# Two tiles of 112 rows in place of two of 128 for each expert, in a DeltaNet layer followed by a mixture of experts

## The chip, the core and the metric

The kernel runs on one core of a Trainium2 chip. A core has five engines that work side by side and meet at semaphores: TensorE (PE; its weight loads are shown apart as PEld), VectorE (DVE), ScalarE (ACT), GpSimd (POOL) and SyncE (SP), which issues most transfers. The metric is device time in microseconds of one execution. The kernel before takes 697.7 us, the median of three runs (694.72, 697.7 and 702.56).

## The reference

The first half is a DeltaNet recurrence over 768 steps for 4 batches of 8 heads of 48 values. Its output, seen as 3072 tokens of 384 values, is `x` of the second half: a gate picks one of 4 groups, a second gate one of the 4 experts of that group, and the token goes through that one expert's two matrices.

```python
# per step t:  y = q_t . state;  state += beta_t * k_t (x) (v_t - k_t . state)   (k normalised)
g_idx = np.argmax(x @ w_group, axis=1)                # 4 groups
e_idx = np.argmax(xg @ w_expert[g], axis=1)           # 4 experts of the group
h  = np.maximum(xg[mask_e] @ w1[g, e], 0.0)           # 384 -> 1024
ye = h @ w2[g, e]                                     # 1024 -> 384
out[tok_idx] = (g_weight * e_weight)[:, None] * ye
```

How many tokens an expert gets depends on the data. Counted from the reference on its inputs, the 16 experts get 203, 162, 176, 211, 203, 190, 203, 201, 181, 200, 183, 224, 195, 202, 155 and 183 tokens.

## The kernel before

**First half.** The recurrence is worked in 24 chunks of 32 steps. Every chunk is a sequence of small matmuls (`gram`, `advance`) with a triangular inverse on DVE beside them (`inverse`), in an order that is written out by hand. `logits` and `route` follow the chunks: they compute the gates, and for each token a slot number. POOL then writes the token's row of 386 values (384 of `x`, the weight of its gate, its row number) by an indirect transfer into the table `x_dram` in device memory (L412). Every expert has a region of that table with room for all tokens; slot numbers count up from the region's first row, so an expert's tokens lie packed at its head. Early in the first half SP writes zeros over the first 256 rows of every region (L498 to L502): a row that no token fills keeps weight 0 and a row number that the last transfer skips.

**Between the halves.** `last` holds where every expert's tokens end; L512 to L519 turn this into the number of 128-row tiles beyond the static ones and their running sum, `tot_i`.

**Second half.** For every expert `take` (L525) fetches the static rows as `xg`, two or three experts ahead, and `experts_rows` (L536) works on them. `STATIC` is 2 here: two tiles of 128 rows.

- L543: PE transposes each tile in three pieces of 128 columns into `t_ps`, and DVE copies it to `xt` (L545).
- L551: the first matrix. The weights are held in the array, 128 columns of `w1` at a time, and both tiles stream past together as 256 columns of `xt`. ACT applies Relu to two such results at a time (L554).
- L558: the second matrix, with the roles exchanged. 128 tokens of `hid` are held, and 384 columns of `w2` stream past; so the two tiles are apart here, with eight matmuls each.
- L561: DVE multiplies by the gate's weight, and POOL sends the rows to their tokens' places by an indirect transfer (L562). It drops rows whose number is out of bounds.

The scheduler moves the transposes ahead: PE transposes the second tile of the next expert and the first tile of the one after it in one go, right behind the last L558 of an expert. The weights of expert e+2 are issued when expert e has used its own (`load_expert`, L102, two buffers each). Every f32 matmul stands in the trace as two MATMUL records and two weight loads; a transpose as one.

**Overflow.** The loop at L577 runs `n_over` times, once for each 128-row tile beyond the static ones: it picks the expert, fetches its weights again, and works on one tile.

Of the kernel before, what the change touches and what calls it, by code (L numbers as in the profile page):

```python
# [9 lines left out]
I32 = mybir.dt.int32  # L10
# [6 lines left out]
RG = 4  # L17
LEAD = 9
ACT_STEP, PE_STEP = "ScalarE", "TensorE"
XW = 386  # L20


def constants(n_tokens, seq, n_experts, n_group, n_batch):

    import numpy as np

    p = np.arange(128)
    i, k = np.meshgrid(np.arange(C), np.arange(C), indexing="ij")
    first = np.arange(n_experts) * n_tokens
    out = {  # L30
        "ident": (p[:, None] == p[None, :]),
        "upper": np.concatenate([(i < k).astype(np.float32)] * n_batch, axis=0),
        "below": np.tile(-(i > k).astype(np.float32).reshape(1, C * C), (128, 1)),
        "before": (p[:, None] < p[None, :]),
        "ones": np.ones((128, 128)),
        "desc": np.tile(np.arange(n_group, 0, -1), (128, RG)),
        "rowid": ((p // C) * seq + p % C)[:, None] - n_tokens,
        "first": (p[:, None] == 0) * first[None, :],
        "tile": np.tile(first // 128, (128, 1)),
        "expert": np.tile(np.arange(n_experts), (128, 1)),  # L40
        "part": p[:, None],
        "tiny": np.full((128, 1), 1e-36),
        "eps": np.full((128, 1), 1e-6),
    }
# [8 lines left out]
def deltanet_then_moe(  # L53
    ctx: ExitStack,
    tc: tile.TileContext,
    const_at: dict,
    shape: tuple,
    kq_d: bass.AP,
    kv_d: bass.AP,
# [28 lines left out]

    x_dram = dp.tile([NE * NS, 128, XW], F32, name="x_dram")

# [20 lines left out]
    with ExitStack() as first:  # L111
# [34 lines left out]
        nc.gpsimd.tensor_copy(acc[:, 0], cut["first"])  # L146
        zero = ap_.tile([128, STATIC * XW], F32, name="zero")
        nc.gpsimd.memset(zero, 0.0)
# [211 lines left out]
        def route(r):  # L360
# [46 lines left out]
            for g, u in enumerate(us):  # L407
                x = xs.pop(u)
                nc.gpsimd.tensor_copy(x[:, DM:DM + 1], cw[:, g])
                for _ in range(2):  # L410
                    yield
                put = nc.gpsimd.indirect_dma_start(  # L412
                    out=x_dram.rearrange("t p d -> (t p) d"),
                    out_offset=bass.IndirectOffsetOnAxis(ap=slot_i[:, g], axis=0),
                    in_=x[:, :], in_offset=None).ins
# [36 lines left out]
        with tc.manual_schedule(engines={mybir.EngineType.PE, mybir.EngineType.DVE,  # L452
# [16 lines left out]
            for u in range(NCH + 1):  # L469
# [28 lines left out]
                if u == 1:  # L498
                    for e in range(NE):
                        nc.sync.dma_start(  # L500
                            out=x_dram[e * NS:e * NS + STATIC].rearrange("t p d -> p t d"),
                            in_=zero.rearrange("p (t d) -> p t d", t=STATIC))  # L502
            while behind:
# [7 lines left out]
        tiles_i = cp.tile([128, NE], I32, name="tiles_i")  # L511
        nc.vector.tensor_scalar(tiles_i, last, 127.0, None, op0=ALU.add)  # L512
        nc.vector.tensor_scalar(tiles_i, tiles_i, 7, None, op0=ALU.arith_shift_right)
        nc.vector.tensor_copy(over, tiles_i)
        nc.vector.tensor_tensor(over, over, cut["tile"], op=ALU.subtract)
        nc.vector.tensor_scalar(over, over, -float(STATIC), 0.0, op0=ALU.add, op1=ALU.max)
        nc.vector.tensor_tensor_scan(out=incl, data0=cut["ones"][:, 0:NE], data1=over,
# [6 lines left out]

    def take(rows, n):  # L525

        xg = mp.tile([128, n, XW], F32, tag=f"xg{n}", name="xg", bufs=3)
        nc.sync.dma_start(out=xg, in_=rows.rearrange("t p d -> p t d"))
        return xg

    def places(xg, n):
        at = mp.tile([128, n], I32, tag=f"at{n}", name="at", bufs=4)
        nc.vector.tensor_scalar(at, xg[:, :, DM + 1], float(N), None, op0=ALU.add)  # L533
        return at

    def experts_rows(xg, T, w1, w2):  # L536

        at = places(xg, T)
# [7 lines left out]
        hid = mp.tile([128, FC, T * 128], F32, tag="hid", name="hid")  # L546
        for f in range(0, FC, 2):
            h_ps = ps.tile([128, 2, T * 128], F32, tag="h", name="h_ps", bufs=3)
            for k in range(2):
                for j in range(DC):  # L550
                    nc.tensor.matmul(h_ps[:, k], lhsT=w1[:, j, (f + k) * 128:(f + k + 1) * 128],  # L551
                                     rhs=xt[:, j], start=(j == 0), stop=(j == DC - 1),
                                     skip_group_check=True)
            nc.scalar.activation(hid[:, f:f + 2], h_ps, ACT.Relu)  # L554
        for i in range(T):
            y_ps = ps.tile([128, DM], F32, tag="o", name="y_ps")
            for f in range(FC):
                nc.tensor.matmul(y_ps, lhsT=hid[:, f, i * 128:(i + 1) * 128], rhs=w2[:, f],  # L558
                                 start=(f == 0), stop=(f == FC - 1))
            yo = mp.tile([128, DM], F32, tag="yo", name="yo", bufs=4)  # L560
            nc.vector.tensor_scalar(yo, y_ps, xg[:, i, DM:DM + 1], None, op0=ALU.mult)  # L561
# [3 lines left out]

    static = lambda e: take(x_dram[e * NS:e * NS + STATIC], STATIC)
    ready = {0: static(0), 1: static(1)}
    for e in range(NE):
        if e + 2 < NE:
            ready[e + 2] = static(e + 2)  # L570
        experts_rows(ready.pop(e), STATIC, *weights.pop(e))
        if e + 2 < NE:
# [4 lines left out]
    with tc.For_i(0, n_over):  # L577
# [6 lines left out]
        nc.vector.tensor_tensor(col, taken, col, op=ALU.subtract)  # L584
        nc.vector.scalar_tensor_tensor(col, in0=ef, scalar=float(NS), in1=col, op0=ALU.mult,
                                       op1=ALU.add)
        pick = mp.tile([128, 2], I32, name="pick")
        nc.vector.tensor_copy(pick[:, 0:1], ef)
        nc.vector.tensor_scalar(pick[:, 1:2], col, float(STATIC), None, op0=ALU.add)
        nc.vector.tensor_scalar(taken, taken, 1.0, None, op0=ALU.add)  # L590
# [3 lines left out]
        cv = nc.values_load(pick[0:1, 1:2], engines=[mybir.EngineType.SP], min_val=0,  # L594
                            max_val=NE * NS - 1,
                            skip_runtime_bounds_check_because="a tile of the sorted tokens")
# [4 lines left out]
        row, used = mp.tile([128, 1], F32, name="row"), mp.tile([128, 1], F32, name="used")  # L601
        nc.vector.tensor_scalar(row, col, float(STATIC), 128.0, op0=ALU.add, op1=ALU.mult)
        nc.vector.tensor_tensor(row, row, cut["part"], op=ALU.add)
        nc.vector.tensor_tensor(used, row, lim, op=ALU.is_lt)
        nc.vector.tensor_scalar(used, used, float(NE * N), None, op0=ALU.mult)
# [11 lines left out]
        experts_rows(take(x_dram[ds(cv, 1)], 1), 1, w1, w2)  # L617

# [44 lines left out]
```

## Time and profile before

| | |
|---|---|
| median of 3 runs | 697.7 us (694.72 to 702.56) |
| the profiled execution | 697.92 us, span 696.1 us |
| PE busy | 549.5 us (79%) |
| PEld busy | 429.6 us (62%) |
| DVE, ACT, POOL busy | 260.0, 138.6, 82.9 us |
| mean granted TensorE clock | 0.904 |
| transfers | 93.53 MB, mean 134 GB/s |

The span is the time from the first to the last instruction of the profiled execution; its own time is 1.8 us longer. "Busy" is the time in which an engine had an instruction under way. Two instructions on PE overlap, so a busy PE doesn't say how fast it goes: that is read from how many instructions of a form lie in how long a stretch. PEclk or "clock" is the share of full speed that TensorE was granted; 1.00 is 2.4 GHz and 0.50 is 1.2 GHz.

### The profile page before, as it was taken

The numbers are of one execution on the slowest core, as the hardware profiler recorded it, in microseconds if no ns is written. First come the engines' busy times: TensorE is split into PE (matmuls) and PEld (weight loads), VectorE is DVE, ScalarE is ACT, GpSimd is POOL, SyncE is SP. The second block draws the span as 40 slices with busy tenths as digits, with TensorE's granted clock in tenths as the row PEclk, the third lists the DMA queues.
The fourth block names the chain that finished last, engine by engine and source line by source line (L and its number), as shares of the span: only waits on it lengthen the run. The fifth ranks groups of instructions, "written<-read, shape, count | busy, mean of one in ns | idle before, by whom it ended". The sixth has DMA issues, their size and how long they took to land. (4 is left out here: it accounts for less than half of the span.)

```text
span 696.1 us, 20147 instructions
## 1 busy us (share of the span) xinstructions
PE 549.5 (79%) x9170; PEld 429.6 (62%) x9170; DVE 260.0 (37%) x773; ACT 138.6 (20%) x233; POOL 82.9 (12%) x152
## 2 busy tenths in 40 slices
PE   2403576777877788861999999999999999999994
PEld 1303465667666677751776677766776677766772
DVE  4399865977859897222111100110001100111000
ACT  1201233343443543320110011101110011100110
POOL 4000000011113103224011100110011100111001
PEclk9999778886868878875999999999999999999997
DMA  9980854233312112103246354553646445463200
GB/s 231 299 251 26 250 170 154 75 93 94 95 48 72 50 48 95 50 14 126 86 159 212 115 205 158 194 181 142 210 135 217 146 178 189 153 217 121 92 5 17
DMA packets 42374, 93.53 MB, mean 134 GB/s; under 512 B 3608, under 2 KB 28362, under 8 KB 42288
## 3 DMA queue, kind: packets, MB, share of 16 engines
q1 hardware_dynamic: 38704, 82.76, 37.0%
q0 software_dynamic: 3584, 9.47, 3.7%
q8 instruction: 72, 1.18, 0.7%
q14 instruction: 14, 0.11, 0.1%
HBM read 76.43 MB, written 17.36 MB: 135 GB/s over the span
## 5 line engine op out<-in xcount | busy, mean ns | idle before, releaser
L551 PE MATMUL h_ps<-xt,w 128*128 128x256 f32 x768 | 170.6, 382 | 8.1 <-DVE xt L545 8.1
L558 PE MATMUL y_ps<-w,hid 128*128 128x384 f32 x512 | 167.7, 486 | 0.0
L551 PEld LDWEIGHTS h_ps<-xt,w 128*128 128x128 f32 x768 | 145.1, 191 | 31.0 <-DVE xt L545 11.7
L558 PEld LDWEIGHTS y_ps<-w,hid 128*128 128x128 f32 x512 | 97.3, 190 | 64.4
L561 DVE TENSOR_SCALAR yo<-y_ps,xg 128x384 f32<-128x384 f32 x32 | 19.7, 617 | 226.3 <-PE y_ps L558 226.3
L554 ACT ACTIVATE hid<-h_ps 128x512 f32<-128x512 f32 x64 | 38.2, 597 | 322.9 <-PE h_ps L551 322.9
L562 POOL DMA_INDIRECT out_dram<-yo,at x32 | 31.5, 983 | 331.2 <-DVE yo L561 327.0
L227 DVE TENSOR_TENSOR m<-m,t 128x30 f32<-128x30 f32 (+9 forms) x180 | 59.5, 330 | 4.5
L223 DVE TENSOR_TENSOR t<-m 128x30 f32<-128x30 f32 (+9 forms) x180 | 59.3, 330 | 4.6
L166 PE MATMUL g_ps<-kqt 48*32 48x64 f32 x1536 | 26.8, 271 | 22.4 <-issue 9.9
L289 ACT ACTIVATE s_bd<-s_ps 48x768 f32<-48x768 f32 x46 | 37.0, 805 | 30.6 <-PE s_ps L282 30.0
L533 DVE TENSOR_SCALAR at<-xg 128x2 int32<-128x2 f32 x16 | 2.7, 168 | 101.5 <-DMA xg<-x_dram 101.5
L282 PE MATMUL s_ps<-w,kv 32*48 32x48 f32 x1472 | 25.9, 227 | 17.1 <-issue 12.3
L355 PE MATMUL l_ps<-wr,xt 128*128 128x20 f32 x144 | 25.0, 304 | 15.7 <-DVE gq L174 10.4
L166 PEld LDWEIGHTS g_ps<-kqt 48*32 48x32 f32 x1536 | 20.7, 129 | 26.6 <-issue 11.8
L271 PE MATMUL w_ps<-f,mt 32*32 32x48 f32 x1472 | 23.1, 213 | 15.9 <-DVE f L259 15.3
L282 PEld LDWEIGHTS s_ps<-w,kv 32*48 32x48 f32 x1472 | 21.7, 134 | 21.2 <-issue 14.2
L293 PE MATMUL o_ps<-w,gq 32*32 32x48 f32 x1536 | 31.8, 250 | 3.1 <-issue 3.1
L255 PE MATMUL a_ps<-s_bd,kqt 128*32 128x96 f32 x736 | 31.9, 337 | 2.5 <-issue 1.7
L355 PEld LDWEIGHTS l_ps<-wr,xt 128*128 128x128 f32 x144 | 22.3, 231 | 18.2 <-DVE gq L174 11.8
L271 PEld LDWEIGHTS w_ps<-f,mt 32*32 32x32 f32 x1472 | 19.5, 112 | 21.5 <-DVE f L259 17.9
L293 PEld LDWEIGHTS o_ps<-w,gq 32*32 32x32 f32 x1536 | 27.2, 141 | 4.5 <-issue 3.6
(92 smaller groups left out, 404.0 us busy)
## 6 DMA issues: line engine op xcount, KB each, us to landing
w<-in_w_dram SPq DMA_DIRECT2D x32, 1536.0 KB, 7.2
kqt<-in_kq_dram SPq DMA_DIRECT2D x48, 192.0 KB, 5.9
kv<-in_kv_dram SPq DMA_DIRECT2D x24, 384.0 KB, 3.4
x_dram<-zero SPq DMA_DIRECT2D x16, 386.0 KB, 8.7
xg<-x_dram SPq DMA_DIRECT2D x16, 386.0 KB, 7.5
con<-in_const_dram SPq DMA_DIRECT2D x1, 754.0 KB, 5.8
out_dram<-yo,at POOLq DMA_INDIRECT x32, 6.2
x_dram<-x,slot_i POOLq DMA_INDIRECT x24, 2.9
```

The lines of the kernel that those rows point to most:

```text
L166: nc.tensor.matmul(g_out[quads[b], hh, j], lhsT=kqt[rows, 0, j, quads[b]], rhs=kqt[rows, :, j, quads[b]], start=True, stop=True, skip_grou ...
L223: nc.vector.tensor_tensor(tv, m[:, j + 1:, j:j + 1].to_broadcast([128, n, j]), m[:, j:j + 1, 0:j].to_broadcast([128, n, j]), op=ALU.mult)
L227: nc.vector.tensor_tensor(m[:, j + 1:, 0:j], m[:, j + 1:, 0:j], tv, op=ALU.add)
L255: nc.tensor.matmul(a_ps[quads[b], 2 * j:2 * j + 2, :], lhsT=kqt[:, 0, j, quads[b]], rhs=s_bd[:, b, j], start=True, stop=True, skip_group_c ...
L271: nc.tensor.matmul(w_ps[b, h], lhsT=mt[b, uu * H + (h % 2) * NP + h // 2], rhs=f[b, h], start=True, stop=True, skip_group_check=True)
L282: nc.tensor.matmul(s_at[hh * 64:hh * 64 + D, b, j], lhsT=k[quads[b], 2 * j + hh], rhs=w[quads[b], 2 * j + hh], start=(u == 0 and j == 0), ...
L289: nc.scalar.activation(s_bd[rows, :, :, hh, :], s_at[rows], ACT.Copy)
L293: nc.tensor.matmul(o_ps[b, h], lhsT=gq[b, h % 2, h // 2], rhs=w[b, h], start=(u == 0 and h == 0), stop=True, skip_group_check=True)
L355: nc.tensor.matmul(l_ps, lhsT=xt[:, j], rhs=wr[:, j], start=(j == 0), stop=(j == DC - 1))
L551: nc.tensor.matmul(h_ps[:, k], lhsT=w1[:, j, (f + k) * 128:(f + k + 1) * 128], rhs=xt[:, j], start=(j == 0), stop=(j == DC - 1), skip_grou ...
L554: nc.scalar.activation(hid[:, f:f + 2], h_ps, ACT.Relu)
L558: nc.tensor.matmul(y_ps, lhsT=hid[:, f, i * 128:(i + 1) * 128], rhs=w2[:, f], start=(f == 0), stop=(f == FC - 1))
```

## The change

Every expert has 224 static slots (`SLOTS`) in place of 256. They are worked as two tiles of `P` = 112 rows. `slots(e)` views them so that partition p holds the slots 2p and 2p+1, one piece of 772 values of the table, where before it held the slots p and 128+p, two pieces of 386. All shapes of `experts_rows` follow from `xg`: the transposes give 112 columns, L551 streams 224, L558 holds 112 tokens and streams 384 columns of `w2` as before.

A region of the table now has `room` = 3200 rows in place of 3072, and the table is addressed in units of 32 rows, since 224 is no multiple of 128. A tile of the overflow loop still has 128 rows, and begins at unit 7 of the region. The number of those tiles is 0 for up to 224 tokens, and 1 for 225 to 352. One small DVE instruction between the halves is gone (L515): the constant `full` takes in what was subtracted twice.

```diff
+SLOTS = 224
-        "tile": np.tile(first // 128, (128, 1)),
+        "full": np.tile(first + SLOTS - 127, (128, 1)),
-    STATIC = -(-N // (NE * 128))
+    T, P = 2, SLOTS // 2
-    x_dram = dp.tile([NE * NS, 128, XW], F32, name="x_dram")
+    x_dram = dp.tile([NE * room // 32, 32, XW], F32, name="x_dram")
+    def slots(e):
+        rows = x_dram[e * room // 32:(e * room + SLOTS) // 32].rearrange("a b d -> (a b) d")
+        return rows.rearrange("(p t) d -> p t d", t=T)
...
-                        nc.sync.dma_start(
-                            out=x_dram[e * NS:e * NS + STATIC].rearrange("t p d -> p t d"),
-                            in_=zero.rearrange("p (t d) -> p t d", t=STATIC))
+                        nc.sync.dma_start(out=slots(e), in_=zero.rearrange("p (t d) -> p t d", t=T))
...
-        nc.vector.tensor_scalar(tiles_i, last, 127.0, None, op0=ALU.add)
+        nc.vector.tensor_tensor(tiles_i, last, cut["full"], op=ALU.subtract)
         nc.vector.tensor_scalar(tiles_i, tiles_i, 7, None, op0=ALU.arith_shift_right)
         nc.vector.tensor_copy(over, tiles_i)
-        nc.vector.tensor_tensor(over, over, cut["tile"], op=ALU.subtract)
-        nc.vector.tensor_scalar(over, over, -float(STATIC), 0.0, op0=ALU.add, op1=ALU.max)
+        nc.vector.tensor_scalar(over, over, 0.0, None, op0=ALU.max)
...
-        xt = mp.tile([128, DC, T * 128], F32, tag="xt", name="xt")
+        xt = mp.tile([128, DC, T * P], F32, tag="xt", name="xt")
         for i in range(T):
-            t_ps = ps.tile([128, DC, 128], F32, tag="t", name="t_ps")
+            t_ps = ps.tile([128, DC, P], F32, tag="t", name="t_ps")
             for j in range(DC):
                 nc.tensor.transpose(out=t_ps[:, j], in_=xg[:, i, j * 128:(j + 1) * 128],
-                                    identity=ident)
-            nc.vector.tensor_copy(xt[:, :, i * 128:(i + 1) * 128], t_ps)
+                                    identity=ident[0:P, 0:P])
+            nc.vector.tensor_copy(xt[:, :, i * P:(i + 1) * P], t_ps)
...
-            h_ps = ps.tile([128, 2, T * 128], F32, tag="h", name="h_ps", bufs=3)
+            h_ps = ps.tile([128, 2, T * P], F32, tag="h", name="h_ps", bufs=3)
...
-            y_ps = ps.tile([128, DM], F32, tag="o", name="y_ps")
+            y_ps = ps.tile([P, DM], F32, tag="o", name="y_ps")
             for f in range(FC):
-                nc.tensor.matmul(y_ps, lhsT=hid[:, f, i * 128:(i + 1) * 128], rhs=w2[:, f],
+                nc.tensor.matmul(y_ps, lhsT=hid[:, f, i * P:(i + 1) * P], rhs=w2[:, f],
                                  start=(f == 0), stop=(f == FC - 1))
```

No instruction changes its place on an engine. PE, one expert and the head of the next, in the order of the program before (the last numbers are output partitions x columns and how many in a row; `w_14` with the lower number behind it is `w1` of expert 14):

```order
L543 MATMUL t_ps<-con,xg 128x128 x6
L551 MATMUL h_ps<-xt,w_14_6790 128x256 x24
L558 MATMUL y_ps<-w_14_6791,hid 128x384 x16
L543 MATMUL t_ps<-con,xg 128x128 x3
L551 MATMUL h_ps<-xt,w_15_6870 128x256 x24
```

And the same place of the change:

```order
L545 MATMUL t_ps<-con,xg 128x112 x6
L553 MATMUL h_ps<-xt,w_14_6791 128x224 x24
L560 MATMUL y_ps<-w_14_6792,hid 112x384 x16
L545 MATMUL t_ps<-con,xg 128x112 x3
L553 MATMUL h_ps<-xt,w_15_6871 128x224 x24
```

The counts stay; the columns that stream past fall in L543 and L551, and in L558 only the output's partitions do.

DVE between the halves before, from the tokens' ends to the first copy of `xt`:

```order
L512 TENSOR_SCALAR tiles_i<-last 128x16
L405 CAST slot_i<-slot 128x4
L513 TENSOR_SCALAR tiles_i<-tiles_i 128x16
L514 CAST over<-tiles_i 128x16
L515 TENSOR_TENSOR over<-over,con 128x16
L516 TENSOR_SCALAR over<-over 128x16
L517 SCALAR_TENSOR_TENSOR incl<-con,over 128x16
L519 CAST tot_i<-incl 128x1
L533 TENSOR_SCALAR at<-xg 128x2
L545 COPY xt<-t_ps 128x3x128
```

And in the change:

```order
L517 TENSOR_TENSOR tiles_i<-last,con 128x16
L412 CAST slot_i<-slot 128x4
L518 TENSOR_SCALAR tiles_i<-tiles_i 128x16
L519 CAST over<-tiles_i 128x16
L520 TENSOR_SCALAR over<-over 128x16
L521 SCALAR_TENSOR_TENSOR incl<-con,over 128x16
L523 CAST tot_i<-incl 128x1
L540 TENSOR_SCALAR at<-xg 112x2
L547 COPY xt<-t_ps 128x3x112
```

One instruction is gone ahead of L517 of before, and the copies have 112 columns a piece.

## Rows read from the trace of the kernel before

**Rows 1.** Windows by stage: us, then each engine's busy us (instructions), clock, transfers.

```profile
0.00:62.00 62.00, 12.01 (x576) 9.07 (x576) 38.55 (x92) 6.98 (x12) 7.45 (x18) 1.00 0.78 219
62.00:326.00 264.00, 190.12 (x7218) 166.02 (x7218) 184.03 (x602) 93.39 (x157) 43.99 (x102) 0.78 0.30 93
326.00:332.00 6.00, 1.79 (x8) 1.44 (x9) 1.08 (x4) 0.00 (x0) 0.00 (x0) 0.50 0.65 202
354.00:686.00 332.00, 323.63 (x1287) 236.83 (x1285) 34.34 (x73) 35.83 (x60) 29.48 (x30) 1.00 0.46 157
686.00:697.00 11.00, 0.00 (x0) 0.00 (x0) 0.39 (x1) 0.00 (x0) 0.98 (x1) 0.62 0.03 9
```

**Rows 2.** Timeline of PE and DVE over one expert: start, length in us, count.

```profile
508.61 0.82 PE L543 MATMUL t_ps<-con,xg 128*128 128x128 f32 x6
509.94 10.63 PE L551 MATMUL h_ps<-xt,w 128*128 128x256 f32 x48 [0.52 <-DVE xt L545]
520.41 10.48 PE L558 MATMUL y_ps<-w,hid 128*128 128x384 f32 x32
530.73 0.49 PE L543 MATMUL t_ps<-con,xg 128*128 128x128 f32 x3
...
508.81 0.62 DVE L561 TENSOR_SCALAR yo<-y_ps,xg 128x384 f32<-128x384 f32 x1 [4.54 <-PE y_ps L558]
509.34 1.01 DVE L545 COPY xt<-t_ps 128x384 f32<-128x384 f32 x2
```

**Rows 3.** Timeline of PE, 511 to 519 us: 39 matmuls of L551.

```profile
510.69 8.58 PE L551 MATMUL h_ps<-xt,w 128*128 128x256 f32 x39
```

**Rows 4.** Groups by line and form, second half: busy us, mean ns, idle before.

```profile
L551 PE MATMUL h_ps<-xt,w 128*128 128x256 f32 x768 | 170.6, 382 | 8.1 <-DVE xt L545 8.1
L558 PE MATMUL y_ps<-w,hid 128*128 128x384 f32 x512 | 167.7, 486 | 0.0
L551 PEld LDWEIGHTS h_ps<-xt,w 128*128 128x128 f32 x768 | 145.1, 191 | 31.0 <-DVE xt L545 11.7
L558 PEld LDWEIGHTS y_ps<-w,hid 128*128 128x128 f32 x512 | 97.3, 190 | 64.4
L554 ACT ACTIVATE hid<-h_ps 128x512 f32<-128x512 f32 x64 | 38.2, 597 | 322.9 <-PE h_ps L551 322.9
L561 DVE TENSOR_SCALAR yo<-y_ps,xg 128x384 f32<-128x384 f32 x32 | 19.7, 617 | 226.3 <-PE y_ps L558 226.3
L545 DVE COPY xt<-t_ps 128x384 f32<-128x384 f32 x32 | 16.4, 548 | 1.2 <-PE t_ps L543 1.2
L357 DVE COPY lg<-l_ps 128x20 f32<-128x20 f32 x24 | 4.2, 176 | 30.6 <-PE l_ps L355 30.5
L516 DVE TENSOR_SCALAR over<-over 128x16 f32<-128x16 f32 x1 | 0.2, 174 | 0.0
```

**Rows 5.** L543: duration min/median/max in ns, first and last start.

```profile
L543 PE MATMUL t_ps<-con,xg x96: 272/273/455, 330.2 to 663.7; 128*128 128x128 f32 x96
```

**Rows 6.** Timeline near 307 us: six weight loads of 128 columns for 20-column matmuls.

```profile
306.99 0.74 PEld L355 LDWEIGHTS l_ps<-wr,xt 128*128 128x128 f32 x6 [0.88 <-ACT xt L351]
```

**Rows 7.** Timeline of SP: the two weight transfers that one expert releases.

```profile
520.60 0.37 SPq L105 DMA_DIRECT2D w<-in_w_dram  x1
530.92 0.37 SPq L106 DMA_DIRECT2D w<-in_w_dram  x1
```

**Rows 8.** Transfers by kind: count, KB each, median us from issue to landing.

```profile
w<-in_w_dram SPq DMA_DIRECT2D x32, 1536.0 KB, 7.2
x_dram<-zero SPq DMA_DIRECT2D x16, 386.0 KB, 8.7
xg<-x_dram SPq DMA_DIRECT2D x16, 386.0 KB, 7.5
out_dram<-yo,at POOLq DMA_INDIRECT x32, 6.2
```

**Rows 9.** Timeline of the zeros' issue (SP), and of what PE waits for then.

```profile
26.43 16.03 SPq L500 DMA_DIRECT2D x_dram<-zero  x15
...
62.72 1.50 PE L271 MATMUL w_ps<-vh,mt 32*32 32x48 f32 x64 [29.12 <-DVE vh L240]
```

**Rows 10.** Timeline between the halves.

```profile
319.37 0.17 DVE L516 TENSOR_SCALAR over<-over 128x16 f32<-128x16 f32 x1
319.65 1.03 POOL L412 DMA_INDIRECT x_dram<-x,slot_i  x1 [2.10 <-DVE over L516]
324.06 0.97 POOL L412 DMA_INDIRECT x_dram<-x,slot_i  x1 [0.28 <-POOL x L409]
326.89 1.41 SPq L528 DMA_DIRECT2D xg<-x_dram  x3
330.06 0.17 DVE L533 TENSOR_SCALAR at<-xg 128x2 int32<-128x2 f32 x1 [10.11 <-DMA xg<-x_dram]
```

**Rows 11.** Timeline of the end.

```profile
685.77 0.62 DVE L561 TENSOR_SCALAR yo<-y_ps,xg 128x384 f32<-128x384 f32 x1 [4.54 <-PE y_ps L558]
686.67 0.98 POOL L562 DMA_INDIRECT out_dram<-yo,at  x1 [4.18 <-DVEq L577]
```

More of the change, by code (lines that the diff above doesn't have):

```diff
@@ L18, with constants @@
 LEAD = 9
+SLOTS = 224
 ACT_STEP, PE_STEP = "ScalarE", "TensorE"
 XW = 386
-def constants(n_tokens, seq, n_experts, n_group, n_batch):
+def constants(n_tokens, seq, n_experts, n_group, n_batch, room):
     import numpy as np
@@ L28, in constants @@
     i, k = np.meshgrid(np.arange(C), np.arange(C), indexing="ij")
-    first = np.arange(n_experts) * n_tokens
+    first = np.arange(n_experts) * room
     out = {
@@ L57, in deltanet_then_moe @@
     shape: tuple,
+    room: int,
     kq_d: bass.AP,
@@ L79, in deltanet_then_moe @@
     NS = N // 128
-    STATIC = -(-N // (NE * 128))
+    T, P = 2, SLOTS // 2
+    assert room % 32 == 0 and SLOTS % 32 == 0 and room >= N + 128
     assert B * C == 128 and NCH % RG == 0
@@ L146, in deltanet_then_moe @@
         nc.gpsimd.tensor_copy(acc[:, 0], cut["first"])
-        zero = ap_.tile([128, STATIC * XW], F32, name="zero")
+        zero = ap_.tile([P, T * XW], F32, name="zero")
         nc.gpsimd.memset(zero, 0.0)
@@ L412, in route @@
                 put = nc.gpsimd.indirect_dma_start(
-                    out=x_dram.rearrange("t p d -> (t p) d"),
+                    out=x_dram.rearrange("a b d -> (a b) d"),
                     out_offset=bass.IndirectOffsetOnAxis(ap=slot_i[:, g], axis=0),
@@ L523, in deltanet_then_moe, with take, experts_rows @@
     ps = ctx.enter_context(tc.tile_pool(name="ps_moe", bufs=2, space=PSUM))
[L525 to L532, printed above, removed]
+    def take(rows):
+        p, t, _ = rows.shape
+        xg = mp.tile([128, t, XW], F32, tag=f"xg{t}", name="xg", bufs=3)
+        nc.sync.dma_start(out=xg[0:p], in_=rows)
+        at = mp.tile([128, t], I32, tag=f"at{t}", name="at", bufs=4)
+        return xg[0:p], at[0:p]
+    def experts_rows(xg, at, w1, w2):
+        P, T, _ = xg.shape
         nc.vector.tensor_scalar(at, xg[:, :, DM + 1], float(N), None, op0=ALU.add)
-        return at
-    def experts_rows(xg, T, w1, w2):
-        at = places(xg, T)
-        xt = mp.tile([128, DC, T * 128], F32, tag="xt", name="xt")
+        xt = mp.tile([128, DC, T * P], F32, tag="xt", name="xt")
         for i in range(T):
-            t_ps = ps.tile([128, DC, 128], F32, tag="t", name="t_ps")
+            t_ps = ps.tile([128, DC, P], F32, tag="t", name="t_ps")
             for j in range(DC):
                 nc.tensor.transpose(out=t_ps[:, j], in_=xg[:, i, j * 128:(j + 1) * 128],
-                                    identity=ident)
-            nc.vector.tensor_copy(xt[:, :, i * 128:(i + 1) * 128], t_ps)
-        hid = mp.tile([128, FC, T * 128], F32, tag="hid", name="hid")
+                                    identity=ident[0:P, 0:P])
+            nc.vector.tensor_copy(xt[:, :, i * P:(i + 1) * P], t_ps)
+        hid = mp.tile([128, FC, T * P], F32, tag="hid", name="hid")
         for f in range(0, FC, 2):
-            h_ps = ps.tile([128, 2, T * 128], F32, tag="h", name="h_ps", bufs=3)
+            h_ps = ps.tile([128, 2, T * P], F32, tag="h", name="h_ps", bufs=3)
             for k in range(2):
@@ L555, in experts_rows @@
         for i in range(T):
-            y_ps = ps.tile([128, DM], F32, tag="o", name="y_ps")
+            y_ps = ps.tile([P, DM], F32, tag="o", name="y_ps")
             for f in range(FC):
-                nc.tensor.matmul(y_ps, lhsT=hid[:, f, i * 128:(i + 1) * 128], rhs=w2[:, f],
+                nc.tensor.matmul(y_ps, lhsT=hid[:, f, i * P:(i + 1) * P], rhs=w2[:, f],
                                  start=(f == 0), stop=(f == FC - 1))
-            yo = mp.tile([128, DM], F32, tag="yo", name="yo", bufs=4)
+            yo = mp.tile([P, DM], F32, tag="yo", name="yo", bufs=4)
             nc.vector.tensor_scalar(yo, y_ps, xg[:, i, DM:DM + 1], None, op0=ALU.mult)
@@ L564, in experts_rows @@
                 in_=yo[:, :], in_offset=None, bounds_check=N - 1, oob_is_err=False)
-    static = lambda e: take(x_dram[e * NS:e * NS + STATIC], STATIC)
-    ready = {0: static(0), 1: static(1)}
+    ready = {0: take(slots(0)), 1: take(slots(1))}
     for e in range(NE):
         if e + 2 < NE:
-            ready[e + 2] = static(e + 2)
-        experts_rows(ready.pop(e), STATIC, *weights.pop(e))
+            ready[e + 2] = take(slots(e + 2))
+        experts_rows(*ready.pop(e), *weights.pop(e))
         if e + 2 < NE:
@@ L584, in deltanet_then_moe @@
         nc.vector.tensor_tensor(col, taken, col, op=ALU.subtract)
-        nc.vector.scalar_tensor_tensor(col, in0=ef, scalar=float(NS), in1=col, op0=ALU.mult,
-                                       op1=ALU.add)
+        nc.vector.tensor_scalar(col, col, 4.0, float(SLOTS // 32), op0=ALU.mult, op1=ALU.add)
+        nc.vector.scalar_tensor_tensor(col, in0=ef, scalar=float(room // 32), in1=col,
+                                       op0=ALU.mult, op1=ALU.add)
         pick = mp.tile([128, 2], I32, name="pick")
         nc.vector.tensor_copy(pick[:, 0:1], ef)
-        nc.vector.tensor_scalar(pick[:, 1:2], col, float(STATIC), None, op0=ALU.add)
+        nc.vector.tensor_copy(pick[:, 1:2], col)
         nc.vector.tensor_scalar(taken, taken, 1.0, None, op0=ALU.add)
@@ L594, in deltanet_then_moe @@
         cv = nc.values_load(pick[0:1, 1:2], engines=[mybir.EngineType.SP], min_val=0,
-                            max_val=NE * NS - 1,
+                            max_val=NE * room // 32 - 4,
                             skip_runtime_bounds_check_because="a tile of the sorted tokens")
@@ L601, in deltanet_then_moe @@
         row, used = mp.tile([128, 1], F32, name="row"), mp.tile([128, 1], F32, name="used")
-        nc.vector.tensor_scalar(row, col, float(STATIC), 128.0, op0=ALU.add, op1=ALU.mult)
+        nc.vector.tensor_scalar(row, col, 32.0, None, op0=ALU.mult)
         nc.vector.tensor_tensor(row, row, cut["part"], op=ALU.add)
         nc.vector.tensor_tensor(used, row, lim, op=ALU.is_lt)
-        nc.vector.tensor_scalar(used, used, float(NE * N), None, op0=ALU.mult)
+        nc.vector.tensor_scalar(used, used, float(NE * room), None, op0=ALU.mult)
         free, zero = mp.tile([128, 1], I32, name="free"), mp.tile([128, XW], F32, name="zero")
@@ L609, in deltanet_then_moe @@
         nc.gpsimd.indirect_dma_start(
-            out=x_dram.rearrange("t p d -> (t p) d"),
+            out=x_dram.rearrange("a b d -> (a b) d"),
             out_offset=bass.IndirectOffsetOnAxis(ap=free, axis=0), in_=zero[:, :],
-            in_offset=None, bounds_check=NE * N - 1, oob_is_err=False)
+            in_offset=None, bounds_check=NE * room - 1, oob_is_err=False)
         w1 = wp.tile([128, DC, F], F32, tag="w1", name="w1_over")
@@ L616, in deltanet_then_moe @@
         nc.sync.dma_start(out=w2, in_=w2_d[ds(ev, 1)].rearrange("o (c p) f -> p (o c) f", p=128))
-        experts_rows(take(x_dram[ds(cv, 1)], 1), 1, w1, w2)
+        rows = x_dram[ds(cv, 4)].rearrange("a b d -> (a b) d")
+        experts_rows(*take(rows.rearrange("(p t) d -> p t d", t=1)), w1, w2)
 def kernel(**inputs):
@@ L642 @@
     wr = np.concatenate([wg, we.transpose(1, 0, 2).reshape(DM, G * Eg)], axis=1)
-    const, const_at = constants(B * S, S, G * Eg, Eg, B)
+    room = -(-(B * S + 128) // 32) * 32
+    const, const_at = constants(B * S, S, G * Eg, Eg, B, room)
     ins = dict(
@@ L659 @@
     with _tile.TileContext(nc) as tc:
-        deltanet_then_moe(tc, const_at, (B, H, S, D), *args)
+        deltanet_then_moe(tc, const_at, (B, H, S, D), room, *args)
     r = _run(nc, [arrays], core_ids=[0])
```

## The prediction

> **What bounds the kernel now.** I read the windows by stage first [rows 1]. Up to 326 us DVE and PE share the first half, and nothing there is changed but the zeros. From 354 to 686 us PE is busy for 323.63 of 332 us at clock 1.00, while DVE, ACT and POOL are busy for a tenth of it each: the second half is PE's, and only what shortens PE's queue there shortens it.
>
> The timeline of one expert [rows 2] shows what an expert costs: the transposes of one begin at 508.61 us, those of the next at 530.73 us, 22.12 us. In it are 48 matmul records of L551 in 10.63 us, 32 of L558 in 10.48 us, and a turn of about 1.3 us (508.61 to 509.94) in which PE transposes and then waits for `xt`.
>
> Mean durations in the groups by line mislead here, since matmuls overlap; the distance from one start to the next is what counts. L551 with 256 columns: 39 starts in 8.58 us [rows 3], the last lasting 0.38 us [rows 4], so (8.58 − 0.38) / 38 = 215.8 ns. L558 with 384 columns: (10.48 − 0.486) / 31 = 322.4 ns [rows 2, 4]. Transposes with 128 columns: (0.82 − 0.273) / 5 = 109 ns [rows 2, 5]. From 256 to 384 columns this is 106.6 ns for 128 columns, 0.833 ns a column; and going down 128 columns from 215.8 gives 109.2 ns, which is what the transposes have. So the distance is a straight line in the columns that stream past, at full clock.
>
> **L551: 256 to 224 columns.** 224 lies between two of those points. 32 columns fewer at 0.833 ns are 26.7 ns, so 215.8 becomes 189.1 ns. There are 768 records [rows 4]: 768 × 26.7 ns = **20.5 us**, all on the path.
>
> Could the weight load become the limit? L551's own record of 128 columns lasts 191 ns [rows 4], just above 189. If a load had to end before the next began, the distance would stay near 191 and the gain would be 768 × 24.8 ns = 19.0 us. But six such loads behind each other for matmuls of 20 columns take 0.74 us [rows 6]: one begins every (0.74 − 0.19) / 5 = 110 ns, so the 191 ns overlap. I take 20.5 and keep 19.0 as an end.
>
> The Trainium skill, "TensorE: Matmul & The Clock Gate", section "Back-to-back issue gap", says that in a stream of weight loads and matmuls the spacing is about 81 ns at 128 columns and 131 ns at 512; by that a column is worth 0.13 ns, 32 of them 4.2 ns, and the sum would be an estimate of 3.2 us in place of 20.5. The rows above have 0.833 ns a column in just such a stream, so I don't use it; what a spacing of that kind would do here is a rival below.
>
> **L558: nothing.** Here the tokens are the held operand. 384 columns of `w2` stream past as before, and 322.4 ns is on the line of columns alone. 112 in place of 128 held columns shorten the load, on which PE does not wait: PEld idles for 64.4 us in this group [rows 4]. Half of the second half's matmul time thus gets nothing from fewer rows. If that cover were gone, the load would come up as a limit only at 190 ns, far under 322.
>
> **The turn between experts.** PE's first matmul of L551 waits for DVE: 8.1 us in all [rows 4], about 0.5 us for each of 15 experts. In rows 2 DVE does `yo` (0.62 us), then two copies, 0.47 us apart in start; PE goes on at 509.94, when the first copy ends (509.34 + 0.55 = 509.89), so the second, which is for the expert after, is hidden. `yo` keeps its 384 values per partition. The copy goes from 384 to 336. Between L357's 20 values in 176 ns and L545's 384 in 548 ns [rows 4] a value costs 372 / 364 = 1.02 ns, so a copy loses 49 ns; 16 × 49 = **0.8 us**. The ends are 0, if something else holds PE, and 1.6, with both copies on the path. The transposes get shorter too, 6 × 13 ns an expert, but the copy then still has `yo` ahead of it on DVE, so I count nothing. Relu on ACT (0.6 us) sits beside PE with 322.9 us to spare [rows 4].
>
> **Between the halves.** The last indirect writes start at 319.65 us, right behind L516 of DVE (319.37 + 0.17) [rows 10]. Without L515 that comes one small instruction earlier, at most 0.2 us (0.17 us by its neighbour L516, rows 4). Then come the first takes: 3.2 us from their issue to the first instruction that reads (326.89 to 330.06). Each moves an eighth less in half as many pieces. Proportion gives 0.4 us less; nothing says that time goes by bytes, so the ends are 0 and 0.4, and the same worse if longer pieces spread badly over the 16 transfer engines. Both together: **0.4 us**, between −0.4 and 0.6.
>
> **Transfers.** SP takes the zeros in 16 us from 26.43 us on, and PE's next wait is for DVE until 62.72 us [rows 9]; they are hidden, whatever they cost. The weights of expert e+2 are released at 520.60 and 530.92 us [rows 7], land in 7.2 us [rows 8], and are used more than 20 us later, after a whole other expert. An expert shorter by 1.3 us takes nothing from that, at a transfer share of 0.46 [rows 1].
>
> **The end.** From the last `yo` at 685.77 us on [rows 11] there is one indirect write of 112 rows in place of 128; I count nothing.
>
> **Sum.** 20.5 + 0.8 + 0.4 = 21.7 us, and 697.92 − 21.7 = **676.2 us**. The profiled execution lies 0.2 us above the median, so against the median of 697.7 this is the same within what the sum can tell. Ends of the terms: 19.0 + 0 − 0.4 = 18.6 and 20.5 + 1.6 + 0.6 = 22.7, so 675.2 to 679.3.
>
> **Rivals.**
>
> *The overflow loop runs once (slower).* The reference's counts have one expert with exactly 224 tokens, the next has 211. The change has room for 224. One more token for that expert on the chip, and the loop, which ran for no tile so far, runs for one. Its price from rows: some nine DVE instructions at 0.17 us to pick the tile (1.6), weights that land in 7.2 us at the earliest, a transpose and a copy (0.9), 48 records of 128 columns at 109 ns (5.2), 16 of L558 at 322 ns (5.2), `yo` and the write (1.6), its landing (6.2) [rows 2, 4, 8, 11]: 28 us. After that wait PE would start at half clock, as between 326 and 332 us at 0.50 [rows 1], which could double the matmuls: 38 us. 676.2 + 28 to 38 gives **704 to 714 us**. It decides at the 225th token. Against it: when I work the reference in double in place of single precision all 16 counts stay, the gates' logits move by 7e-8, and the token nearest to joining that expert is 3e-4 away. Chance 2%.
>
> *The distance goes only partly by the columns.* If the load's 110 ns [rows 6] were a fixed share of every 215.8 ns, only the other 106 ns would shrink with the columns: 32/256 × 106 = 13 ns, 768 × 13 = 10.2 us, and 697.92 − 10.2 − 1.2 = **686.5 us**. If something else spaced the starts altogether, nothing would be left of L551's term: 697.92 − 1.2 = **696.7 us**. Three points on one line speak against both, since a fixed share would lift the transposes above 109 ns. Chance 1% each.
>
> The section "Back-to-back issue gap" of the Trainium skill's page "TensorE: Matmul & The Clock Gate" would lie between these two: with its estimate of 3.2 us it would be some 693.5 us.
>
> *The first half moves.* Its work is the same, yet its clock is 0.78 on the mean and its zeros land elsewhere [rows 1, 9]. The three runs of before, with the same work throughout, lie 3.0 us under and 4.9 us over their median. So much can hide or add to the gain without the change having to do with it: 676.2 − 3.0 to 676.2 + 4.9, **673 to 681 us**. It is a spread about the forecast more than a case against it; that it exceeds this and takes more than half of the gain I give 2%.
>
> *The weight load limits L551*, within the forecast: 677.7 us.
>
> **How the numbers follow.** The forecast, with the limits of its terms, has 94%; the overflow loop 2%, the columns' rival 1% for a part and 1% for none, a first half that eats the gain 2%. The range takes the ends of the terms (675.2 to 679.3) and the spread of the runs, about half of it added at either end beyond the terms, since both extremes seldom meet: **672 to 682 us**. About 1% is what a measurement of this kernel can tell from no change; faster than 690.7 us is forecast with 95%, within 1% with 3%, slower than 704.7 us with 2%.
>
> **What will show it.** In the profile after: L551 with 224 columns has 48 records in about 9.3 us (47 × 189 ns and the last), so starts 189 ns apart; L558 keeps 10.48 us for 32; from one expert's transposes to the next's are 20.8 us; the copies take 0.50 us; PE's clock from 354 us on is 1.00; the first half ends within the runs' spread of 326 us; and no instruction of the overflow loop is there. The forecast is wrong if L551's starts stay more than 195 ns apart, if L558's change at all, if PE begins to wait for `xg` or weights, or if the loop's lines show up.

## The result, and the profile after

The change takes 674.62 us, the median of four runs (671.28 to 681.42), where the kernel before had 698.75 us in four: a ratio of 0.964, interval 0.956 to 0.972. The ratio leaves out the run of 681.42 us, which is more than 1.5% above the fastest; by the medians of all four runs it is 0.965. Six more runs on another occasion (674.6 to 681.66 us) gave 676.94 us and 0.974, interval 0.969 to 0.978. The forecast was 676.2 us, in a range of 672 to 682.

The profiled execution is the fastest of the first four runs (671.28 us), with a span of 669.5 us. First the timeline of PE and DVE over one expert (start and length in us, count), which answers to [rows 2].

```profile
513.58 0.74 PE L545 MATMUL t_ps<-con,xg 112*128 112x112 f32 x6
514.87 9.35 PE L553 MATMUL h_ps<-xt,w 128*128 128x224 f32 x48 [0.55 <-DVE xt L547]
524.05 10.48 PE L560 MATMUL y_ps<-w,hid 128*112 128x384 f32 x32
534.37 0.74 PE L545 MATMUL t_ps<-con,xg 112*128 112x112 f32 x6
...
513.78 0.62 DVE L563 TENSOR_SCALAR yo<-y_ps,xg 112x384 f32<-112x384 f32 x1 [4.54 <-PE y_ps L560]
514.31 0.91 DVE L547 COPY xt<-t_ps 128x336 f32<-128x336 f32 x2
```

From transposes to transposes are 20.79 us, where there were 22.12: 1.33 us less. 1.29 us of it lie between the first start of the first matrix and that of the second (9.18 us, before 10.47), and 0.04 us in the turn. L560 has the 10.48 us that L558 had, to the hundredth, with 112 tokens in place of 128.

A stretch of L553 alone, which answers to [rows 3]:

```profile
515.73 7.54 PE L553 MATMUL h_ps<-xt,w 128*128 128x224 f32 x39
```

(7.54 − 0.35) / 38 = 189.2 ns from start to start; 189.1 was forecast. The groups by line, which answer to [rows 4]:

```profile
L560 PE MATMUL y_ps<-w,hid 128*112 128x384 f32 x512 | 167.7, 486 | 0.0
L553 PE MATMUL h_ps<-xt,w 128*128 128x224 f32 x768 | 151.2, 357 | 8.5 <-DVE xt L547 8.5
L553 PEld LDWEIGHTS h_ps<-xt,w 128*128 128x128 f32 x768 | 145.3, 192 | 12.0 <-DVE xt L547 11.7
L560 PEld LDWEIGHTS y_ps<-w,hid 128*112 128x112 f32 x512 | 90.6, 177 | 70.0
L547 DVE COPY xt<-t_ps 128x336 f32<-128x336 f32 x32 | 14.8, 499 | 1.1 <-PE t_ps L545 1.1
```

PEld's idle time ahead of L553 fell from 31.0 to 12.0 us, and what is left is the wait for `xt`. A load's record (192 ns) now lasts slightly longer than the distance between matmul starts (189.2 ns); that it still doesn't hold them up is shown by the run with 192 slots below. L560's loads got shorter, 177 ns for 190, and only their idle time grew.

The windows of the first half and of most of the second answer to [rows 1]:

```profile
62.00:326.00 264.00, 185.36 (x7227) 160.52 (x7227) 185.56 (x605) 93.47 (x157) 44.00 (x102) 0.79 0.31 97
354.00:660.00 306.00, 297.33 (x1254) 223.52 (x1252) 31.94 (x70) 31.56 (x58) 27.27 (x29) 1.00 0.48 163
```

PE's clock is 1.00 again in the second half. Between the halves, and at the end, little moved [rows 10, 11]:

```profile
312.48 0.17 DVE L517 TENSOR_TENSOR tiles_i<-last,con 128x16 int32<-128x16 f32 x1
312.68 0.17 DVE L412 CAST slot_i<-slot 128x4 int32<-128x4 f32 x1
313.66 1.03 POOL L419 DMA_INDIRECT x_dram<-x,slot_i  x1 [2.10 <-DVE incl L521]
...
320.83 1.27 SPq L533 DMA_DIRECT2D xg<-x_dram  x3
324.02 0.17 DVE L540 TENSOR_SCALAR at<-xg 112x2 int32<-112x2 f32 x1 [10.27 <-DMA xg<-x_dram]
...
659.32 0.62 DVE L563 TENSOR_SCALAR yo<-y_ps,xg 112x384 f32<-112x384 f32 x1 [4.54 <-PE y_ps L560]
```

The same first two instructions in the profile of before:

```profile
318.48 0.16 DVE L512 TENSOR_SCALAR tiles_i<-last 128x16 int32<-128x16 f32 x1
318.67 0.17 DVE L405 CAST slot_i<-slot 128x4 int32<-128x4 f32 x1
```

The first takes need 3.2 us from issue to first use, as before. From the last `yo` to the end of the span are 10.2 us (10.3 before).

The span fell by 26.6 us, and this divides in two at one landmark: the first of the small DVE instructions on the tokens' ends, L512 of before, L517 now. From it to the end of the span were 696.1 − 318.5 = 377.6 us, and now there are 669.5 − 312.5 = 357.0: 20.6 us less. The other 6.0 us lie ahead of the landmark, in the first half, where the change has only the zeros and the places of the rows in the table. What they are is the first question of the experiments.

### The profile page after: what moved, and what is told of

Same layout as the page of the kernel before. It is cut to its first block, busy times and chain, and to the rows that moved or that the text cites. A ratio compares the mean times of both kernels' runs of the same rounds, so it can differ in the third digit from the quotient of the medians.

```text
span 669.5 us, 20146 instructions
## 1 busy us (share of the span) xinstructions
PE 522.2 (78%) x9170; PEld 415.3 (62%) x9170; DVE 258.4 (39%) x772; ACT 135.3 (20%) x233; POOL 81.5 (12%) x152
## 3 DMA queue, kind: packets, MB, share of 16 engines
q8 instruction: 72, 1.18, 0.7%
## 5 line engine op out<-in xcount | busy, mean ns | idle before, releaser
L560 PE MATMUL y_ps<-w,hid 128*112 128x384 f32 x512 | 167.7, 486 | 0.0
L553 PE MATMUL h_ps<-xt,w 128*128 128x224 f32 x768 | 151.2, 357 | 8.5 <-DVE xt L547 8.5
L553 PEld LDWEIGHTS h_ps<-xt,w 128*128 128x128 f32 x768 | 145.3, 192 | 12.0 <-DVE xt L547 11.7
L560 PEld LDWEIGHTS y_ps<-w,hid 128*112 128x112 f32 x512 | 90.6, 177 | 70.0
L563 DVE TENSOR_SCALAR yo<-y_ps,xg 112x384 f32<-112x384 f32 x32 | 19.8, 618 | 203.6 <-PE y_ps L560 203.6
L556 ACT ACTIVATE hid<-h_ps 128x448 f32<-128x448 f32 x64 | 34.8, 544 | 305.8 <-PE h_ps L553 305.8
L564 POOL DMA_INDIRECT out_dram<-yo,at x32 | 30.1, 941 | 312.0 <-DVE yo L563 307.8
L540 DVE TENSOR_SCALAR at<-xg 112x2 int32<-112x2 f32 x16 | 2.7, 169 | 105.6 <-DMA xg<-x_dram 105.6
L173 PEld LDWEIGHTS g_ps<-kqt 48*32 48x32 f32 x1536 | 20.4, 127 | 26.0 <-issue 11.7
L278 PE MATMUL w_ps<-f,mt 32*32 32x48 f32 x1472 | 23.0, 214 | 16.6 <-DVE f L266 15.7
L262 PE MATMUL a_ps<-s_bd,kqt 128*32 128x96 f32 x736 | 29.8, 317 | 6.1 <-issue 4.4
L362 PEld LDWEIGHTS l_ps<-wr,xt 128*128 128x128 f32 x144 | 22.4, 231 | 19.2 <-DVE gq L181 13.4
L278 PEld LDWEIGHTS w_ps<-f,mt 32*32 32x32 f32 x1472 | 19.5, 114 | 22.4 <-DVE f L266 18.4
L300 PE MATMUL o_ps<-w,gq 32*32 32x48 f32 x1536 | 28.9, 234 | 2.0 <-issue 1.9
L419 POOL DMA_INDIRECT x_dram<-x,slot_i x24 | 24.6, 1024 | 35.0 <-DVE t L230 17.9
```

Source lines behind the costliest of these rows:

```text
L173: nc.tensor.matmul(g_out[quads[b], hh, j], lhsT=kqt[rows, 0, j, quads[b]], rhs=kqt[rows, :, j, quads[b]], start=True, stop=True, skip_grou ...
L262: nc.tensor.matmul(a_ps[quads[b], 2 * j:2 * j + 2, :], lhsT=kqt[:, 0, j, quads[b]], rhs=s_bd[:, b, j], start=True, stop=True, skip_group_c ...
L278: nc.tensor.matmul(w_ps[b, h], lhsT=mt[b, uu * H + (h % 2) * NP + h // 2], rhs=f[b, h], start=True, stop=True, skip_group_check=True)
L362: nc.tensor.matmul(l_ps, lhsT=xt[:, j], rhs=wr[:, j], start=(j == 0), stop=(j == DC - 1))
L560: nc.tensor.matmul(y_ps, lhsT=hid[:, f, i * P:(i + 1) * P], rhs=w2[:, f], start=(f == 0), stop=(f == FC - 1))
L564: nc.gpsimd.indirect_dma_start(out=out[:, :], out_offset=bass.IndirectOffsetOnAxis(ap=at[:, i:i + 1], axis=0), in_=yo[:, :], in_offset=Non ...
```

## The experiments

**The change once more** (no edit).

> The change once more, unaltered, for a second profile and more times. In the first profile the second half was shorter by what the columns give (22.12 to 20.79 us for each expert), and the first half besides ended 6.0 us earlier than in the profile of before. Theory A, the first half's end is a spread of the clock that has nothing to do with the change: the distance from one expert to the next is 20.79 us again to 0.02 us, while the first half's end (the start of the small DVE instructions on the tokens' ends, 318.5 us before and 312.5 us in the first profile of the change) falls anywhere from 308 to 323 us; median ratio to before 0.965 to 0.972. Theory B, the change shortens the first half by some 6 us through its smaller zeros: the first half ends at 312 to 314 us again, ratio 0.958 to 0.965.

Measured: 676.94 us, ratio 0.974 (0.969 to 0.978). The landmark is at 317.3 us, and from it to the end of the span (673.3 us) are 356.0 us: 21.6 less than before. The experts are 20.79 us apart:

```profile
496.63 0.74 PE L545 MATMUL t_ps<-con,xg 112*128 112x112 f32 x6
517.42 0.74 PE L545 MATMUL t_ps<-con,xg 112*128 112x112 f32 x6
```

So the second half repeats, and the 6.0 us do not: with the same instructions the first half ended 4.8 us later than in the first profile. The ratio lies just above Theory A's figures, into which its interval reaches, and its interval excludes Theory B's.

**The new layout with 256 slots.**

```diff
-SLOTS = 224
+SLOTS = 256
```

> The change with 256 slots: the new layout of the table (one piece of 772 values for each partition in place of two of 386, regions of 3200 rows, one DVE instruction less), but 256 columns for L553 and the zeros' bytes of before. Theory A, only the columns count: 22.12 us for each expert as before, and the time of before within 0.5%, ratio 0.995 to 1.003. Theory B, the layout gives the first half 6 us: ratio 0.990 to 0.993, its first half ending at 312 to 314 us and the experts at 22.12 us. If the copies' pieces at the first takes matter, they show between the last indirect write and the first transpose: 5.15 us before, within 0.5 us of that by either theory.

Measured: 697.65 us, ratio 1.001 (0.9985 to 1.0035). Timeline of PE over one expert:

```profile
508.93 0.82 PE L545 MATMUL t_ps<-con,xg 128*128 128x128 f32 x6
510.27 10.63 PE L553 MATMUL h_ps<-xt,w 128*128 128x256 f32 x48 [0.52 <-DVE xt L547]
520.74 10.48 PE L560 MATMUL y_ps<-w,hid 128*128 128x384 f32 x32
531.06 0.82 PE L545 MATMUL t_ps<-con,xg 128*128 128x128 f32 x6
```

22.13 us, as before. One piece of 772 values in place of two of 386, the larger regions and the missing DVE instruction are worth nothing that can be measured in the time. All of the gain is in the number of slots.

**192 slots**, with nine overflow tiles.

```diff
-SLOTS = 224
+SLOTS = 192
```

> The change with 192 slots, two tiles of 96: nine experts have more than 192 tokens, so the overflow loop runs for nine tiles. Two things are read. First the distance of L553's starts with 192 columns: by the line of columns 192 x 0.833 + 2.4 = 162.4 ns and 19.4 us for each expert; if a weight load's record of 190 ns were a floor, it stays at 190 ns and 20.8 us for each expert; if the load's 110 ns were a fixed share, 189 ns at 224 columns would have been 202 ns already, so that is out. Second the price of an overflow tile: 28 to 38 us each by the prediction's rival, so 250 to 340 us for nine and 900 to 1000 us in all; if the loop overlaps one tile's weights with the next one's work, under 25 us each.

Measured: 949.59 us, one run. The timeline of PE: an expert's transposes and a stretch of L553 with 192 columns in the static part, and a stretch with 128 columns in the overflow loop, at full clock.

```profile
512.93 0.66 PE L545 MATMUL t_ps<-con,xg 96*128 96x96 f32 x6
...
514.75 5.53 PE L553 MATMUL h_ps<-xt,w 128*128 128x192 f32 x33
...
706.43 3.18 PE L553 MATMUL h_ps<-xt,w_over 128*128 128x128 f32 x27
```

(5.53 − 0.33) / 32 = 162.5 ns at 192 columns, on the line and well under the 190 ns that a weight load's record lasts in this run too: the load's record as a limit is out. The experts are 19.46 us apart, where 19.4 was expected. At 128 columns (3.18 − 0.28) / 26 = 111.5 ns, where the line gives 109. That the pace of the loads themselves begins to show here is likely: the last four of the six loads of [rows 6] begin 111 to 112 ns apart, though only 20 columns stream past between them. No run with fewer columns in this place shows it apart. The nine tiles cost 288 us (947.8, less the last static matmul's start at 648.8, less the 10.7 us that end the change without a loop), 32 us each.

**One overflow tile**, as if one expert had a 225th token.

```diff
-        "full": np.tile(first + SLOTS - 127, (128, 1)),
+        "full": np.tile(first + SLOTS - 128, (128, 1)),
```

> The change with the constant of the overflow count one lower (SLOTS - 128 in place of SLOTS - 127), so that the one expert with exactly 224 tokens is given an overflow tile, in which no row is a token's: the case of the slower rival, a 225th token. Prediction's price: 28 us, or 38 us with TensorE at half clock behind the wait, so 704 to 714 us and a ratio of 1.007 to 1.022 to before. If the loop is cheaper than the chain of its parts, under 20 us and still faster than before (ratio under 0.995).

Measured: 706.83 us, ratio 1.012 (1.007 to 1.018): about 1% slower than before. In its profile the last static matmul starts at 666.6 us and the span ends at 706.0, 39.4 us later; without the loop it is 10.7 us. So the tile costs 28.7 us. The last static matmuls, then SP and PE in the timeline of the loop:

```profile
663.69 3.39 PE L560 MATMUL y_ps<-w,hid 128*112 128x384 f32 x10
...
670.32 0.39 SPq L618 DMA_DIRECT2D w_over<-in_w_dram  x1
670.95 0.38 SPq L619 DMA_DIRECT2D w_over<-in_w_dram  x1
678.31 0.35 SPq L533 DMA_DIRECT2D xg<-x_dram  x1
681.96 0.90 PE L545 MATMUL t_ps<-con,xg 128*128 128x128 f32 x3 [14.89 <-DMA xg<-x_dram]
683.52 7.72 PE L553 MATMUL h_ps<-xt,w_over 128*128 128x128 f32 x48 [0.65 <-DVE xt L547]
691.07 5.33 PE L560 MATMUL y_ps<-w_over,hid 128*128 128x384 f32 x16
```

PE waits for the tile's rows, not for the weights. SP's waits in the same profile (us in all, times, the longest) name what holds the take at 678.31, the indirect write that clears the tile's unused rows:

```profile
SPq L533 <- DMA x_dram<-zero,free: 6.4, 1, 6.4
```

The take itself needs another 3.6 us. And PE begins the tile at half clock, as the rival's upper price had it, but only for its first 6 us (1.00 from 688 us on):

```profile
681.96:687.80 5.84, 5.19 (x23) 4.79 (x24) 0.69 (x2) 0.38 (x1) 0.00 (x0) 0.50 0.00 0
```

So L553 took 7.6 us (683.52 to 691.07), where the lower price counts 5.2. Against this stands the landing of the output, 6.2 us of the price, which is in the 10.7 us of the end anyhow. The rival's lower sum (28 us) thus came out by luck: its chain had the wrong wait, and errors of opposite sign made up for each other.

**Streaming the tokens in the second matrix too.** If L558 gets nothing because the tokens are the held operand, exchanging the roles should bring the gain there as well.

```diff
+            if late and f in (2, 4):
+                late.pop(0)()
-        for i in range(T):
-            y_ps = ps.tile([P, DM], F32, tag="o", name="y_ps")
+        yt = mp.tile([128, DC, T * P], F32, tag="yt", name="yt")
+        for c in range(DC):
+            z_ps = ps.tile([128, T * P], F32, tag="o", name="z_ps")
             for f in range(FC):
-                nc.tensor.matmul(y_ps, lhsT=hid[:, f, i * P:(i + 1) * P], rhs=w2[:, f],
+                nc.tensor.matmul(z_ps, lhsT=w2[:, f, c * 128:(c + 1) * 128], rhs=hid[:, f],
                                  start=(f == 0), stop=(f == FC - 1))
+            nc.scalar.activation(yt[:, c], z_ps, ACT.Copy)
...
+            y_ps = ps.tile([P, DM], F32, tag="b", name="y_ps", bufs=1)
+            for c in range(DC):
+                nc.tensor.transpose(out=y_ps[:, c * 128:(c + 1) * 128],
+                                    in_=yt[:, c, i * P:(i + 1) * P], identity=ident)
```

The transposes back are called from within the next expert's first matrix, behind the second and the third of its four steps (`late`); `xg` has a fourth buffer for that.

> The change with the roles of the second matrix exchanged: 128 columns of w2 are held and the 224 token columns of hid stream past (48 records of 224 columns in place of 32 of 384), ACT copies the three results, PE turns them back by six transposes an expert, put between the next expert's matmuls of the first matrix. If only streamed columns count, the second matrix takes 48 x 189 ns = 9.07 us in place of 10.32, the six transposes add 0.6 to 0.7 us, and yo no longer stands ahead of the copy of xt, which takes up to 0.5 us off the turn between experts, against a wait for ACT's last copy of up to 0.5 us: 19.7 to 20.2 us for each expert in place of 20.79, so 9 to 17 us less than the change in the second half, and a ratio to before of 0.945 to 0.962. Rival: the held operand was never the point, what is saved in columns goes into transposes and waits: 20.6 us or more for each expert and the ratio of the change, 0.968 to 0.975.

Measured: 668.9 us, six runs, beside 704.71 us for before on that occasion: ratio 0.950 (0.947 to 0.953). Timeline of PE:

```profile
518.14 0.45 PE L546 MATMUL t_ps<-con,xg 112*128 112x112 f32 x3
518.43 0.64 PE L571 MATMUL y_ps<-con,yt 128*112 128x128 f32 x3
518.90 0.45 PE L546 MATMUL t_ps<-con,xg 112*128 112x112 f32 x3
519.19 7.07 PE L554 MATMUL h_ps<-xt,w 128*128 128x224 f32 x36
526.10 0.49 PE L571 MATMUL y_ps<-con,yt 128*112 128x128 f32 x3
526.43 2.44 PE L554 MATMUL h_ps<-xt,w 128*128 128x224 f32 x12
528.70 9.24 PE L564 MATMUL z_ps<-hid,w 128*128 128x224 f32 x48
537.78 0.45 PE L546 MATMUL t_ps<-con,xg 112*128 112x112 f32 x3
```

19.64 us for each expert: the second matrix has 9.08 us from its first start to the next transposes (10.32 in the change), and PE no longer waits for `xt`, since transposes fill the turn. One half of an expert's transposes back stands where it is called (526.10 us); the other was moved ahead, into that turn (518.43 us). This is the fastest version here.

**The same, turned back at once.** The transposes stand directly behind the expert's own matmuls.

> The same exchange of roles, but with the six transposes back directly behind the expert's own matmuls, ahead of the next expert's. The same 9.07 us for the second matrix; but the third piece of each tile waits for ACT's copy of the last result (0.4 us) and the second tile for yo to free the only buffer (0.6 us), with nothing of the next expert's first matrix in between: 20.6 to 21.2 us for each expert, no better than the change's 20.79. If it comes out under 20.2 us as well, the place of the transposes doesn't matter.

Measured: 679.76 us in one run, on the same occasion; 20.32 us for each expert, less than I expected. The scheduler put some of the next expert's transposes between, so that only the wait for `yo` was left.

```profile
500.73 0.38 PE L567 MATMUL y_ps<-con,yt 128*112 128x128 f32 x2
...
521.05 0.38 PE L567 MATMUL y_ps<-con,yt 128*112 128x128 f32 x2
...
PE y_ps L567 <- DVE yo L570: 5.9, 16, 0.7
```

(The last line is of the waits of PE: us in all, times, the longest.) The place of the transposes is worth 0.68 us an expert.

**Both matrices streaming, with 256 slots.** The edit is `SLOTS = 256` again.

> The exchange of roles (stream_both, 19.65 us for each expert) with 256 slots in two tiles of 128. If a matrix whose tokens stream pays for every column, and one whose tokens are held pays for none, then here both matrices pay: 2 x 48 x 26.7 ns = 2.56 us more than stream_both, and the copy 0.05, so 22.2 to 22.3 us for each expert, as slow as the kernel before (22.12), ratio 0.997 to 1.008. The exchange is then worth something only with the fewer slots. Rival: the exchange gains by itself, through the turn between experts alone: under 21.7 us for each expert and a ratio under 0.99.

Measured: 707.76 us, beside 699.51 us for before on that occasion: ratio 1.011 (1.007 to 1.016), about 1% slower than before. Timeline of PE:

```profile
521.57 0.49 PE L571 MATMUL y_ps<-con,yt 128*128 128x128 f32 x3
521.89 2.76 PE L554 MATMUL h_ps<-xt,w 128*128 128x256 f32 x12
524.49 10.52 PE L564 MATMUL z_ps<-hid,w 128*128 128x256 f32 x48
...
543.86 0.49 PE L571 MATMUL y_ps<-con,yt 128*128 128x128 f32 x3
```

22.29 us for each expert: 2.65 us more than with 224 slots, twice what the change itself gained. A matrix whose tokens stream pays for every slot, one whose tokens are held paid for none. The exchange alone costs 0.17 us an expert, and some 5 us at the end, where nothing covers the last transposes: 16.1 us from the last matmul of the second matrix to the end of the span, 10.9 before. The ratio is above what I had expected by that end.

## Why the prediction was right, point by point

- **L551.** Forecast 26.7 ns a record and 20.5 us. Measured 215.8 to 189.2 ns, 26.6 ns less, 20.4 us for 768 records at full clock. With 192 columns the line held on (162.5 ns), which refutes the other ends (a load's record as a floor, a fixed share).
- **L558 nothing.** Right to 0.01 us an expert; the exchange of roles and its repeat with 256 slots show the cause.
- **The turn.** Forecast 0.8 us by a copy 49 ns shorter; the copy fell from 548 to 499 ns, and the turn by 0.04 us an expert, 0.6 us in all.
- **Between the halves, and the end.** Forecast 0.4 us. In the first profile 0.3 us from the landmark to the first matmul of L553 and 0.1 us behind the last `yo`; with 256 slots 0.1 us in each place. So the figure fits, by luck, for neither part of the forecast came true. POOL's first write starts 1.18 us behind the landmark with one DVE instruction less, where it was 1.17 us, and the first takes need 3.2 us as before. The prediction read the write as waiting for L516, which ended just ahead of it; but the write reads `slot_i`, and it starts 0.98 us behind the start of the cast that makes `slot_i` in both kernels (318.67 to 319.65 us, 312.68 to 313.66 us). The instruction that is gone stood behind that cast.
- **Transfers and zeros.** No new wait of PE for `xg` or weights. Nothing shows a gain from smaller zeros.
- **The sum.** 21.7 us. From the landmark to the end: 20.6 and 21.6 us in the two profiles. The difference lies in the first expert, which ran partly at half clock (0.50 from 326.14 to 329.40 us in the first profile, from 330.94 to 332.20 us in the second) and took 22.4 us in the one and 21.4 in the other (first start of L553 to the next expert's), 22.7 before. I had counted 1.33 us for it as for the other 15; it gave 0.3 and 1.3.
- **The first half.** The spread was named. The landmark lies at 318.5 us in the profile of before, and at 312.5 (the change), 317.3 (the change once more), 318.3 (256 slots), 321.3 (one overflow tile) and 324.1 us (192 slots); in the three kernels whose second matrix streams the tokens too it is at 321 to 327 us. The windows from 62 us to the landmark, for before, the change, and the change once more:

```profile
62.00:318.48 256.48, 190.12 (x7218) 166.02 (x7218) 182.75 (x595) 93.39 (x157) 39.46 (x95) 0.78 0.30 93
62.00:312.48 250.48, 183.54 (x7218) 159.02 (x7218) 183.26 (x594) 93.47 (x157) 39.48 (x95) 0.80 0.30 95
62.00:317.26 255.26, 193.18 (x7218) 166.87 (x7218) 183.31 (x594) 93.21 (x157) 39.12 (x95) 0.80 0.30 93
```

  In the first profile of the change PE was busy with the same 7218 records for 6.6 us less than before, about as much as the first half was shorter (6.0 us); but the repeat had PE busy for 3.1 us more than before and ended 1.2 us earlier all the same. The clock, 0.80 in both, doesn't tell the two apart. PE's first matmul of the recurrence (L271, now L278) starts at 62.7 to 63.1 us in these three profiles and at 65.8 to 67.3 us in the others, so that some of their delay arises ahead of it. What sets the end of the first half is not settled, and that it is what moved the medians is argued from single profiles.
- **Luck in the number.** The first median, 674.62 us, lies 1.6 us under the forecast and the second, 676.94 us, 0.7 us over it. With a first half that ended 4.8 us apart in two executions of the same kernel, such closeness is partly chance: the profiled execution, 671.28 us, lies below the range, and would lie in it without those 6 us. What the prediction got right by its reasons is the second half.
- **The slower rival** was priced at 28 to 38 us and costs 28.7; it didn't happen, since no tile of the loop ran.

## What to carry to other kernels

Ask for every matmul which operand streams and which is held: cutting rows shortens only the matmuls in which they stream, and there, in these runs, in a straight line from 256 down to 192 columns. A measured line through two or three sizes in the trace prices a cut better than a share of the mean duration of overlapping records: an eighth of L551's 382 ns would be 48 ns a record, and a record gave 26.6. And a static size cut down to the largest count of one data set gains 21 us here, but the first token beyond it costs 29.

## What the runs showed of the hardware that was not expected

The six transposes of an expert take 0.74 us with 112 rows, (0.74 − 0.26) / 5 = 96 ns apart, where they were 109 ns apart with 128. That is on the line, since 112 columns stream past in them. Not expected was that their weight loads keep up: a load of `xg` in L545 has 128 columns of 112 rows, and such loads follow each other 96 ns apart too, closer than the 110 ns of [rows 6]. With 96 rows the transposes are (0.66 − 0.25) / 5 = 82 ns apart. So a load of 128 columns is not held to 110 ns there; whether that is due to its fewer rows or to the matmul behind it, no run here tells apart.
